# Relative-position attention plus a gated MLP: keys of a head split over the two row halves, scores and transposes in 64-row tiles, double-bank copies, another order

## The chip, the cores and the metric

The kernel runs on one core of a Trainium2 chip. The metric is the device time of one execution in microseconds (us). The profile is one execution of the same program; its time is the span from its first to its last instruction. The engines are named as the profile names them: PE (TensorE matmuls), PEld (TensorE weight loads), DVE (VectorE), ACT (ScalarE), POOL (GpSimd) and SP (the queue that issues most DMAs).

## The reference, cut to what matters

```python
# q, k, v: (8 batches, 8 heads, 576, 64) float32
scores = q @ k^T / 8
x = log1p(|i - j|) / log1p(max(i, 1))              # 576 x 576
scores += (relu(x * w1 + b1) @ w2)[head]           # a bias per head
attn = exp(scores - rowmax); attn /= rowsum + 1e-9
y = attn @ v                                       # -> 4608 tokens x 512
out = ((y @ W1) * (y @ W2)) @ W3 @ W_out           # 512 -> 1024 -> 1024 -> 512
```

All is float32. W3 and W_out are multiplied with each other once (the fold), so that the MLP is an up part (two products) and a down part (one). To get float32 results from one-pass matmuls, an operand is split into a rounded part and a rest (h and l), and a product is the sum of terms such as h*h + h*l + l*h.

## The kernel before, in words

**Stages.** A prologue makes the bias of all heads and stores it in DRAM (nb_d); attention runs over 32 units (4 head pairs times 8 batches, u = 8 * pair + batch); the fold multiplies W3 by W_out; the MLP runs over 9 chunks of 512 tokens. Stages overlap at their ends. While attention runs, W3 and W_out are converted in 24 pieces (steps c0 to c7, units with batch 1 to 6); W1 and W2 are converted in 16 pieces after it.

**One unit** has nine score tiles: 0 to 7 (head h = t mod 2, query rows 128*(t div 2) and on) and M, whose 128 rows are the last 64 query rows of both heads. Its steps, each on one engine:

- ld (SP): raw q, k and v are loaded. g (POOL): q and k are split into h and l parts. gq makes Q, gk makes K and kl.
- S (PE): a tile's 128 x 576 scores, in a PSUM tile `s` of two banks, 288 columns in each; two such tiles exist.
- T (DVE): scores plus bias `nb`, scaled, into `ts`, with the row extreme `mx`. E (ACT): exp into `pp`, with the row sum.
- F (PE): transposes of `pp`, 128 x 128 each, into a PSUM tile `pst`; four one-bank tiles exist. H (DVE or ACT): copies out of `pst` into `pt` and `px`. L and N are the remaining corners.
- r (DVE): reciprocals of the row sums, each unit, transposed in N, stored to DRAM by SP (rd).
- W0, W1 (PE): value products for queries 0 to 255 and 256 to 575, with 64-column tiles: the two heads lie in the two column halves. X: their copies out of PSUM. xd (SP): the unit's result to DRAM.

**Order.** A table (ORDER) gives each step of unit u a time u * PERIOD + t; sorted, this is the order in which PE, DVE, ACT and POOL issue. Each engine runs its list in order and waits at the front. SP's list is sorted by the framework. So a unit's S, the F of the unit before and the W of an earlier one are interleaved. The fold and the MLP are placed the same way after `t_s`, the time of the last S or E.

In `scores` one tile half takes two matmuls: Q holds the h part of q on rows 0 to 63 and the l part on rows 64 to 127, K and kl hold the h and l part of k on both halves, so that all 128 rows add up (h + l) * (h + l).

Of the kernel before, what the change touches and what calls it, by code (L numbers as in the profile page):

```python
# [55 lines left out]
def arrange(NU, pieces):

    at = {n: (t, e) for e, steps in ORDER.items() for n, t in steps.items()}
    at["rd"] = at["HN"][0] + 0.8, "SP"
    at["xd"] = max(at["X0"][0], at["X1"][0]) + 0.8, "SP"  # L60
    at["c0"] = at["c1"][0] - 4.8, "SP"
    at["c7"] = max(at["c2"][0], at["c6"][0]) + 0.6, "POOL"
    return {(n, u): (u * PERIOD + t if u or n not in FIRST else FIRST[n], e) for u in range(NU) for n, (t, e) in at.items() if n[0] != "c" or u in pieces}


@with_exitstack
def relpos_attention_moe(
# [133 lines left out]

    Q2 = []
    for i in range(2):
        qt = qk.tile([P, 2 * (S + P)], F32R, name=f"Q{i}")
        nc.gpsimd.memset(f(qt[:, S:S + P]), 0.0)
        Q2.append(qt)

# [40 lines left out]
    def op_g(u, n):  # L248

        d = st[u]  # L250
        x = d.pop("r" + n)
        if n == "q":
            Q = Q2[u % 2]
            Qd = halves(Q)[:, :, 0:S]
            x = halves(x)
# [1 line left out]
            nc.gpsimd.tensor_tensor(Qd[hi], x[hi], f(Qd[hi]), op=ALU.subtract)
            d["Q"] = Q
        else:
            K = qk.tile([P, 2 * S], F32R, name="K", bufs=2)  # L260
            kl = qk.tile([P, 2 * S], F32R, name="kl", bufs=2)
            nc.gpsimd.tensor_scalar(K, x, 1.0, 1.0, op0=ALU.mult, op1=ALU.mult)
            nc.gpsimd.tensor_tensor(kl, x, f(K), op=ALU.subtract)
            d.update(K=K, kl=kl)

    def op_S(u, t):
# [1 line left out]
        Q, K, kl = d["Q"], d["K"], d["kl"]
        d["s", t] = ps_s.tile([P, 2, 512], F32, name="s")
        for hf in range(2):  # L270
            scores(d["s", t][:, hf, :HS], t, hf, Q, K, kl)

    def scores(s, t, hf, Q, K, kl):
        js = slice(hf * HS, (hf + 1) * HS)
        if t == "M":

            l, m = Q[:, 512:512 + P], Q[:, S + 64:S + 64 + P]
            ops = [(s, l, x[:, js]) for x in (K, kl)]
            if hf == 0:
                ops += [(s, m, x[:, S + 64:S + 64 + HS]) for x in (K, kl)]  # L280
            else:
                ops += [(s[:, 0:512 - HS], m, x[:, S + 64 + HS:2 * S]) for x in (K, kl)]
                ops += [(s[:, 512 - HS:HS], m, x[:, S:S + 64]) for x in (K, kl)]
# [526 lines left out]
```

## Time and profile before

| | |
|---|---|
| time, median of 3 runs | 1242.14 us (1241.1 to 1243.2) |
| span of the profiled execution | 1241.4 us |
| PE busy | 1200.8 us, 97% of the span, 7136 matmuls |
| PEld / DVE / ACT / POOL busy | 956.6 / 656.6 / 603.5 / 390.0 us |
| mean granted TensorE clock | 0.989 |

A row of groups reads: line, engine, operation, output<-inputs, shapes, count | busy time in all, mean ns of one | idle time of the engine ahead of them, and what ended it. A row of the timeline reads: start, length (us), engine, line, operation, count, and in brackets the idle time ahead and what ended it; the length of a matmul or a weight load holds its way through the array, so the distance from one start to the next says how long it holds the engine. A row of stretches reads: from:to, length, then busy time and count of PE, PEld, DVE, ACT and POOL, granted clock, DMA share, GB/s.

### The profile page before, as it was taken

How to read it: one execution, taken by the hardware profiler on the slowest of the kernel's cores; microseconds unless marked ns; L12 is line 12 of the kernel's file. 1: busy time of each engine (PE TensorE's matmuls, PEld its weight loads, DVE VectorE, ACT ScalarE, POOL GpSimd, SP SyncE). 2: the span in 40 equal slices, each digit the busy share in tenths (PEclk: the TensorE clock that was granted, in tenths of full speed). 3: DMA queues.
4: the chain of work that ended last, by engine and by line, in shares of the span. 5: the costliest groups of instructions: out<-in, count | busy, mean ns of one | idle time of the engine just before them, and what ended most of it. 6: DMA issues, size and time to landing. Idle time of an engine off the chain costs nothing. (4 is left out here: it accounts for less than half of the span.)

```text
span 1241.4 us, 19015 instructions
## 1 busy us (share of the span) xinstructions
PE 1200.8 (97%) x7136; PEld 956.6 (77%) x7136; DVE 656.6 (53%) x1380; ACT 603.5 (49%) x1303; POOL 390.0 (31%) x260
## 2 busy tenths in 40 slices
PE   7679999999999999999989999999999999999998
PEld 3168887777778887887768788888888888888887
DVE  8647776777677767776999532222222131313111
ACT  7558887888788877888544321212121212121211
POOL 0436664666456655661654300000000000000000
PEclk9879999999999999999999999999999999999999
DMA  7854446444645463431443220212111110200001
GB/s 215 286 172 143 144 149 204 133 142 145 220 133 152 152 219 120 148 94 54 135 132 117 68 74 29 68 34 65 38 51 51 51 51 35 68 34 1 29 7 34
DMA packets 60795, 130.25 MB, mean 105 GB/s; under 512 B 8992, under 2 KB 18592, under 8 KB 60704
## 3 DMA queue, kind: packets, MB, share of 16 engines
q1 hardware_dynamic: 59408, 127.32, 32.7%
q10 hardware_dynamic: 1296, 1.72, 0.5%
q8 instruction: 56, 0.92, 0.3%
q14 instruction: 35, 0.29, 0.1%
HBM read 99.10 MB, written 29.92 MB: 104 GB/s over the span
## 5 line engine op out<-in xcount | busy, mean ns | idle before, releaser
L298 DVE CUSTOM_DVE_ANT_0 ts<-s,nb 128x576 f32<-128x576 f32 x256 | 184.7, 749 | 148.1 <-ACT pt L363 74.1
L661 PE MATMUL up<-xh,wl 128*128 128x512 f32 x576 | 225.4, 391 | 0.1
L669 DVE TENSOR_TENSOR g<-up,a 128x512 f32<-128x512 f32 x72 | 49.7, 690 | 332.2 <-PE up L661 332.2
L661 PE MATMUL up<-xh,wh 128*128 128x512 f32 x576 | 225.3, 391 | 0.0
L661 PE MATMUL up<-xl,wh 128*128 128x512 f32 x576 | 225.3, 391 | 0.0
L290 PE MATMUL s<-K,Q 128*128 128x288 f32 (+2 forms) x672 | 206.0, 326 | 16.2 <-DVE mx L298 7.6
L321 ACT ACTIVATE pp<-ts,mx 128x576 f32<-128x576 f32 x256 | 196.7, 770 | 39.2 <-DVE mx L298 39.1
L290 PE MATMUL s<-kl,Q 128*128 128x288 f32 (+2 forms) x672 | 182.1, 295 | 0.0
L686 PE MATMUL o<-w3s,gh 128*128 128x512 f32 x576 | 177.8, 390 | 0.0
L666 ACT COPY a<-up 128x512 f32<-128x512 f32 x72 | 42.2, 586 | 247.5 <-PE up L661 247.5
L647 POOL TENSOR_SCALAR xh<-xr 128x512 fp32r<-128x512 f32 x36 | 23.9, 664 | 435.7 <-DVE xr L643 432.5
L290 PEld LDWEIGHTS s<-K,Q 128*128 128x128 f32 x672 | 128.3, 191 | 38.2 <-DVE mx L298 18.0
L355 PE MATMUL pst<-ident,pp 128*128 128x128 f32 x1024 | 152.8, 278 | 0.0
L363 ACT ACTIVATE pt<-pst 128x512 f32<-128x512 f32 x224 | 129.5, 594 | 34.2 <-PE pst L355 29.9
L397 PE MATMUL pst<-pt,rv 128*64 128x320 f32 (+1 forms) x1024 | 138.3, 412 | 0.0
L355 PEld LDWEIGHTS pst<-ident,pp 128*128 128x128 f32 x1024 | 118.8, 141 | 15.2 <-DVE wi L148 11.8
L672 ACT ACTIVATE gh<-g 128x512 fp32r<-128x512 f32 x72 | 45.5, 632 | 172.8 <-DVE g L669 172.8
L290 PEld LDWEIGHTS s<-kl,Q 128*128 128x128 f32 x672 | 129.0, 192 | 0.0
L661 PEld LDWEIGHTS up<-xh,wl 128*128 128x128 f32 x576 | 108.2, 188 | 23.9 <-DVE wl L582 0.5
L661 PEld LDWEIGHTS up<-xl,wh 128*128 128x128 f32 x576 | 108.3, 188 | 23.3
L661 PEld LDWEIGHTS up<-xh,wh 128*128 128x128 f32 x576 | 108.3, 188 | 23.2
L686 PEld LDWEIGHTS o<-w3s,gh 128*128 128x128 f32 x576 | 108.2, 188 | 22.8
(85 smaller groups left out, 1720.3 us busy)
## 6 DMA issues: line engine op xcount, KB each, us to landing
rk<-in_k_dram SPq DMA_DIRECT2D x31, 576.0 KB
rq<-in_q_dram SPq DMA_DIRECT2D x31, 576.0 KB
wi<-in_moe_w_dram SPq DMA_DIRECT2D x32, 512.0 KB
nb_d<-bev SPq DMA_DIRECT2D x36, 295.5 KB
rv<-in_v_dram SPq DMA_DIRECT2D x32, 320.0 KB
x_d<-x SPq DMA_DIRECT2D x32, 288.0 KB
xr<-x_d SPq DMA_DIRECT2D x36, 256.0 KB
rb<-r_d SPq DMA_DIRECT2D x72, 128.0 KB
```

The costliest lines, as they stand in the source:

```text
L290: nc.tensor.matmul(o, l, r, start=(m == 0), stop=(m == len(ops) - 1))
L298: nc.vector.tensor_tensor_reduce(out=halves(ts), in0=d.pop(("s", t))[:, :, :HS], in1=halves(NB[p, t]), op0=ALU.add, op1=ALU.min, scale=-1. ...
L321: nc.scalar.activation(pp, ts, AF.Exp, bias=mx, scale=-1.0, accum_out=d["sum"][:, col:col + 1])
L355: nc.tensor.transpose(ps[:, c * P:(c + 1) * P], x, ident)
L363: nc.scalar.activation(o, x, AF.Copy)
L397: nc.tensor.matmul(acc[rows], x[:, c0:c0 + D], m, start=(c == 0), stop=(c == 4))
L647: nc.gpsimd.tensor_scalar(xh, xr, 1.0, 1.0, op0=ALU.mult, op1=ALU.mult)
L661: nc.tensor.matmul(acc, l[:, cc], r, start=(n == 0), stop=(n == 3 * NC - 1))
L666: nc.scalar.copy(a, ps[0])
L669: nc.vector.tensor_tensor(g, ps[1], a, op=ALU.mult)
L672: nc.scalar.activation(gh, g, AF.Copy)
L686: nc.tensor.matmul(d["o", t], l[:, sl], folded[ft][r], start=(ft == 0 and n == 0), stop=(ft == NF - 1 and n == 2),)
```

## The change

**Operands.** k is no longer doubled: of a head's 576 keys the first 288 lie on rows 0 to 63, the others on rows 64 to 127 (raw k is 128 x 576 in place of 128 x 1152). q lies on both halves, h and l in tiles of their own, with each head padded to 640 columns (128 x 1280). There is one raw buffer of each, where there were two.

**Scores.** A tile is three terms (qh*kh, ql*kh, qh*kl; M six), and each term is two matmuls: rows 0 to 63 write the first bank, rows 64 to 127 the second. The term l*l is left out.

**Transposes.** Each 128 x 128 block is turned by two matmuls of 64 rows, one per bank. `pst` is a two-bank tile; there are two. F0 to F3 turn both heads of a query block (16 matmuls), FL what lies past column 512, FN a corner. H copies 1024 columns at once. W0 and W1 share a `pst` tile from W0's start to X, which is now on DVE.

**Other work.** Row sums of a pair's 8 units are kept in one tile; r, its transpose (R) and its 16 small DMAs come once per pair. In every conversion piece the clamp goes from DVE to POOL and the `rest` step from ACT to POOL. ORDER, PERIOD, the number of buffers and the pace of the fold are others: X and HN follow T7 on DVE, W1 of a unit stands three periods behind its first score tile, the first unit begins with tiles 6 and M.

TensorE at the end of W's neighbourhood, before: a score tile's second half and the next one, transposes, W1 (`s` scores, `pst` transposes or value products).

```order
L290 MATMUL s<-K,Q_121 128x288
L290 MATMUL s<-kl,Q_121 128x288
L290 MATMUL s<-K,Q_121 128x288
L290 MATMUL s<-kl,Q_121 128x288
L355 MATMUL pst<-ident,pp 128x128 x4
L397 MATMUL pst<-pt_857,rv 64x320 x8
L397 MATMUL pst<-px_858,rv 64x320 x2
```

The same place now: F0, S0, W1.

```order
L321 MATMUL pst<-ident,pp 128x64 x16
L266 MATMUL s<-kh,qh 128x288 x2
L266 MATMUL s<-kh,ql 128x288 x2
L266 MATMUL s<-kl,qh 128x288 x2
L386 MATMUL pst<-pt_858,rv 64x320 x8
L386 MATMUL pst<-pt_858,rv 64x256
L386 MATMUL pst<-px_859,rv 64x64
L386 MATMUL pst<-pt_858,rv 64x256
L386 MATMUL pst<-px_859,rv 64x64
```

Four full-row matmuls of a score tile have become three pairs of half-row ones, four transposes sixteen shorter ones, and W1's last part is cut in two.

TensorE further on, now: S4, FN, F3. F3 reuses the `pst` tile that W0 and W1 of another unit filled.

```order
L266 MATMUL s<-kh,qh 128x288 x2
L266 MATMUL s<-kh,ql 128x288 x2
L266 MATMUL s<-kl,qh 128x288 x2
L328 MATMUL pst<-ident,ppM_861 128x64
L329 MATMUL pst<-ident,ppM_861 128x64
L321 MATMUL pst<-ident,pp 128x64 x16
```

F3 thus stands behind the X that empties that tile; ahead of it PE has nothing else in its list.

VectorE around the corner copies (`px`), before (`ts,mx<-s` is a T, its second row reads the row extreme):

```order
L361 COPY pt_859<-pst 128x8x64
L298 ISA ts,mx<-s,nb_4117 128x576
L298 ISA mx 128x1
L298 ISA ts,mx<-s,nb_4167 128x576
L298 ISA mx 128x1
L361 COPY px_860<-pst 64x64 x2
L361 COPY rt<-pst 9x128
L134 TENSOR_SCALAR wmag<-wmag 128x512
```

and now, from T7 to HL:

```order
L277 ISA ts,mx<-s,nb_4623 128x576
L277 ISA mx 128x1
L344 COPY x<-pst 128x256
L344 COPY x<-pst 128x320
L344 COPY px_857<-pst 64x64 x2
L277 ISA ts,mx<-s,nb_4665 128x576
L277 ISA mx 128x1
L277 ISA ts,mx<-s,nb_4763 128x576
L277 ISA mx 128x1
L344 COPY pt_856<-pst 128x2x4x128
```

The two copies of X stand behind T7, HN and T4 behind X; the clamp (L134) has left this list.

```diff
-AT_F, PACE_F = 2.00, 2.80
+AT_F, PACE_F = 2.50, 3.20
-AT_W1, PACE_W, AT_X, PACE_X = 4.00, 5.70, 24.00, 2.10
+AT_W1, PACE_W, AT_X, PACE_X = 4.00, 5.70, 37.00, 2.10
-PERIOD = 15.82
+PERIOD = 13.21
-        "S0": 0.00, "S1": 1.66, "S2": 2.64, "S3": 4.31, "S4": 5.18, "S5": 8.31, "S6": 8.84, "F0": 9.37, "F1": 12.87,
+        "S6": 0.00, "SM": 0.40, "S5": 1.75, "S7": 5.79, "S4": 6.19, "S3": 7.68, "S2": 9.48, "S1": 9.88, "S0": 15.85,
...
+AT_R = 23.41
-NPP, NTS, NPS = 6, 3, 4
+NPP, NTS, NPS = 7, 4, 2
...
         def rest():
-            nc.scalar.activation(x, d["lo"].bitcast(U32), AF.Copy, scale=2.0 ** -52)
+            nc.gpsimd.tensor_scalar(x, d["lo"].bitcast(U32), 2.0 ** -52, 1.0, op0=ALU.mult, op1=ALU.mult)
 
         def clamp():
-            nc.vector.tensor_scalar(d["mag"], d["mag"], LEAST, MOST, op0=ALU.max, op1=ALU.min)
+            nc.gpsimd.tensor_scalar(d["mag"], d["mag"], LEAST, MOST, op0=ALU.max, op1=ALU.min)
...
-    raw = att_r.enter_context(tc.tile_pool(name="raw", bufs=2, side="right"))
+    raw = att_r.enter_context(tc.tile_pool(name="raw", bufs=1, side="right"))
...
+        h = qk.tile([P, x.shape[1]], F32R, name=f"{n}h", bufs=2)
+        l = qk.tile([P, x.shape[1]], F32R, name=f"{n}l", bufs=2)
+        nc.gpsimd.tensor_scalar(h, x, 1.0, 1.0, op0=ALU.mult, op1=ALU.mult)
+        nc.gpsimd.tensor_tensor(l, x, f(h), op=ALU.subtract)
+        d[n] = (h, l)
+
+    TERMS = ((0, 0), (1, 0), (0, 1))
...
-            ops = [(s, l, x[:, h * S + hf * HS:h * S + (hf + 1) * HS]) for x in (K, kl)]
-        for m, (o, l, r) in enumerate(ops):
-            nc.tensor.matmul(o, l, r, start=(m == 0), stop=(m == len(ops) - 1))
+            ops = [(h, h * SQW + i * P, x, y) for x, y in TERMS]
+        for m, (h, q0, x, y) in enumerate(ops):
+            for hf, rows in enumerate((lo, hi)):
+                nc.tensor.matmul(
+                    s[:, hf, :HS], Q[x][rows, q0:q0 + P], K[y][rows, h * HS:(h + 1) * HS],
+                    start=(m == 0), stop=(m == len(ops) - 1),
+                )
...
-            nc.vector.tensor_scalar(r, d["sum"], 1e-9, None, op0=ALU.add)
-            nc.vector.reciprocal(r, r)
+            nc.vector.tensor_scalar(sums[p], sums[p], 1e-9, None, op0=ALU.add)
+            nc.vector.reciprocal(sums[p], sums[p])
...
+    def turn(ps, c0, x):
+        for hf, rows in enumerate((lo, hi)):
+            n = x.shape[1]
+            nc.tensor.transpose(ps[0:n, hf, c0:c0 + 64], x[rows], ident[rows, rows])
 
     def op_F(u, n):
         d = st[u]
-        ps = ps_t.tile([P, 512], F32, name="pst")
+        ps = d["F" + n] = ps_t.tile([P, 2, 512], F32, name="pst")
...
+            for c in range(4):
+                for h in range(2):
+                    c0 = h * (S + 64) + c * P
+                    turn(ps, (2 * c + h) * 64, d["P", int(n)][:, c0:c0 + P])
...
     def op_W(u, n):
...
-        acc = ps_t.tile([P, 512], F32, name="pst")[:, 0:n_q]
+        if "acc" not in d:
+            d["acc"] = ps_t.tile([P, 2, 512], F32, name="pst")
+        acc = d["acc"][:, int(n), 0:qs.stop - qs.start]
```

More of the change, by code (lines that the diff above doesn't have):

```diff
@@ L56, in arrange @@
 def arrange(NU, pieces):
     at = {n: (t, e) for e, steps in ORDER.items() for n, t in steps.items()}
[L59 to L63, printed above, removed]
+    at.update(r=(max(at["E" + t][0] for t in TILES) + 1.0, "DVE"), R=(AT_R, "PE"), HR=(AT_R + 0.85, "DVE"), rd=(AT_R + 1.3, "SP"))
@@ L66, in relpos_attention_moe @@
+    at["xd"] = max(t for n, (t, _) in at.items() if n[0] == "X") + 0.8, "SP"
+    at["c0"] = min(at["c1"][0], at["c2"][0]) - 4.4, "SP"
+    return {(n, u): (u * PERIOD + t if u or n not in FIRST else FIRST[n], e) for u in range(NU) for n, (t, e) in at.items() if (n[0] != "c" or u in pieces) and (n not in ("r", "R", "HR", "rd") or u % 8 == 7)}
 @with_exitstack
@@ L195, in relpos_attention_moe @@
     lo, hi = slice(0, 64), slice(64, 128)
-    NB = {}
+    NB, sums, rts = {}, {}, {}
     st = {u: {"P": [None] * 9} for u in range(NU)}
[L202 to L206, printed above, removed]
     def halves(x):
@@ L238, in load @@
         else:
-            t = raw.tile([P, 2 * S], F32, name=f"r{which}")
+            t = raw.tile([P, src.shape[3]], F32, name=f"r{which}")
         queue = nc.scalar if u == 0 and which != "v" else nc.sync
@@ L266, in op_S @@
+        l = qk.tile([P, x.shape[1]], F32R, name=f"{n}l", bufs=2)
[3 more added lines that the diff above has]
+    TERMS = ((0, 0), (1, 0), (0, 1))
     def op_S(u, t):
         d = st[u]
[L268 to L274, printed above, removed]
-        if t == "M":
[L277 to L283, printed above, removed]
+        Q, K = d["q"], d["k"]
+        s = d["s", t] = ps_s.tile([P, 2, 512], F32, name="s")
+        if t == "M":
+            ops = [(h, h * SQW + 512, x, y) for h in range(2) for x, y in TERMS]
@@ L310, in op_E @@
         ts, mx = d.pop(("t", t))
-        if "sum" not in d:
-            d["sum"] = sm.tile([P, 9], F32, name="sum", bufs=3)
+        p, b = units[u]
+        if p not in sums:
+            sums[p] = sm.tile([P, 9 * B], F32, name="sum")
         if t == "M":
-            pp, col = ppool.tile([P, S], F32, name="ppM", bufs=2), 8
-            d["PM"] = pp
+            pp, col = PM2[u % 2][:, 64:64 + S], 8
         else:
@@ L395, in op_W @@
                 c0 = (4 * h + c if c < 4 else 8 + h) * D
-                m = PT[:, c, h * S + qs.start:h * S + qs.stop] if c < 4 else PX[:, qs]
-                nc.tensor.matmul(acc[rows], x[:, c0:c0 + D], m, start=(c == 0), stop=(c == 4))
+                if c < 4:
+                    ms = [(acc[rows], PT[:, 2 * c + h, qs])]
+                else:
+                    k0, k1 = qs.start // 64, min(qs.stop, 512) // 64
+                    w = (k1 - k0) * 64
+                    ms = [(acc[rows, 0:w].rearrange("p (k j) -> p k j", j=64), PT[:, k0:k1, S:SQW])]
+                    if qs.stop == S:
+                        ms.append((acc[rows, w:], PX))
+                for n_m, (o, m) in enumerate(ms):
+                    nc.tensor.matmul(
+                        o, x[:, c0:c0 + D], m, start=(c == 0), stop=(c == 4 and n_m == len(ms) - 1),
+                    )
         d["acc" + n] = acc
@@ L401, in op_X @@
         d = st[u]
-        if "x" not in d:
-            d["x"] = sm.tile([P, S], F32, name="x")
-        move(on, (d["x"][:, QS[int(n)]], d["acc" + n]))
+        d["x"] = sm.tile([P, S], F32, name="x")
+        move(on, *((d["x"][:, qs], d["acc"][:, m, 0:qs.stop - qs.start]) for m, qs in enumerate(QS)))
     def op_x(u, n):
@@ L549, in relpos_attention_moe @@
     ps_t = att.enter_context(tc.tile_pool(name="ps_t", bufs=NPS, space=PSUM))
-    PTX = [(pt.tile([P, 4, 2 * S], F32, name=f"pt{i}"), pt.tile([P, S], F32, name=f"px{i}")) for i in range(2)]
+    PTX = [(pt.tile([P, 8, SQW], F32, name=f"pt{i}"), pt.tile([P, 64], F32, name=f"px{i}")) for i in range(2)]
+    PM2 = [ppool.tile([P, S + P], F32, name=f"ppM{i}") for i in range(2)]
+    for x in PM2:
+        for c0 in (0, 64 + S):
+            nc.gpsimd.memset(x[:, c0:c0 + 64], 0.0)
     drive([e for e in later if e[0] < t_s])
```

119 lines of the change are left out of this document (54 added, 65 removed), and 5 rows, old and new, of the table ORDER.

## The prediction, made before the changed kernel had run

> **What bounds the kernel now.** I read the stretches first, to see which engine is full in which stage, then the timeline of TensorE in one unit, then the rows of the engines that empty its results.
>
> ```profile
> core 0: 1241.4 us, clock 0.989
> 100.00:200.00 100.00, 99.28 (x784) 80.91 (x783) 74.55 (x184) 79.96 (x185) 61.58 (x37) 1.00 0.55 169
> 580.00:640.00 60.00, 54.40 (x273) 40.83 (x268) 53.49 (x69) 32.74 (x62) 31.38 (x23) 1.00 0.49 142
> 640.00:710.00 70.00, 69.04 (x301) 55.92 (x300) 59.80 (x80) 29.13 (x50) 32.21 (x25) 1.00 0.31 98
> ```
>
> In attention PE is busy for 99.28 of 100 us at full clock, DVE 74.55, ACT 79.96, POOL 61.58: PE alone sets the pace. In the fold (580 to 710) DVE is nearly as full as PE. From 710 on the MLP runs; the change does not touch it.
>
> ```profile
> 300.83 1.95 PE L397 MATMUL pst<-pt,rv 128*64 128x256 f32 x16
> 303.14 0.40 PE L290 MATMUL s<-K,Q 128*128 128x288 f32 x1
> 304.82 2.38 PE L397 MATMUL pst<-pt,rv 128*64 128x320 f32 x16
> 307.67 0.66 PE L355 MATMUL pst<-ident,pp 128*128 128x128 f32 x4
> 309.05 0.38 PE L290 MATMUL s<-K,Q 128*128 128x288 f32 x1
> 309.27 0.30 PE L290 MATMUL s<-kl,Q 128*128 128x288 f32 x1
> 309.40 0.29 PE L290 MATMUL s<-K,Q 128*128 128x288 f32 x1
> 315.92 0.27 PE L342 MATMUL pst<-ident,ppM 128*64 128x128 f32 x1
> 316.03 0.27 PE L343 MATMUL pst<-ident,ppM 128*128 128x128 f32 x1
> 573.65 1.95 PE L397 MATMUL pst<-pt,rv 128*64 128x256 f32 x16
> ```
>
> From start to start: W0 holds PE for 2.31 us, W1 for 2.85, a 288-column score matmul for 0.133 (0.22 as the first after another kind), a transpose for 0.11. From one unit's W0 (300.83) to that of the 17th unit after it (573.65) are 272.82 us: **16.05 us a unit**.
>
> **The change on PE.** A score tile goes from four turns to three pairs. If the two halves of a pair run side by side, it takes 3 x 0.133 = 0.40 us in place of 0.53; all nine (M is double) 4.0. No row of before has 64-row tiles, so this is the first unknown. The nearest rows are those of column halves:
>
> ```profile
> L397 PEld LDWEIGHTS pst<-pt,rv 128*64 128x64 f32 x1024 | 67.8, 136 | 48.8 <-issue 10.5 <-PE wacc L619 0.4
> 57.09 0.23 PE L517 MATMUL bacc<-zact,w2b 128*32 128x16 f32 x1
> 57.10 0.23 PE L517 MATMUL bacc<-zdve,w2b 128*32 128x16 f32 x1
> 309.40 0.19 PEld L290 LDWEIGHTS s<-kl,Q 128*128 128x128 f32 x1
> 310.04 0.19 PEld L290 LDWEIGHTS s<-K,Q 128*128 128x128 f32 x1
> 310.15 0.19 PEld L290 LDWEIGHTS s<-kl,Q 128*128 128x128 f32 x1
> 310.29 0.42 PEld L355 LDWEIGHTS pst<-ident,pp 128*128 128x128 f32 x4
> L355 PEld LDWEIGHTS pst<-ident,pp 128*128 128x128 f32 x1024 | 118.8, 141 | 15.2 <-DVE wi L148 11.8 <-issue 3.4
> L342 PEld LDWEIGHTS pst<-ident,ppM 128*64 128x64 f32 x32 | 3.5, 110 | 0.0
> ```
>
> The value products load 1024 times 136 ns, 139 us, in 67.8 us of busy time: two column halves load at once. Column tiles also start their matmuls 0.01 us apart. The load at 309.40 begins with the matmul of the same rows at 309.40: the next weights come in while the array works. So I take side by side for row halves too. Bounds: one after the other would cost 0.11 to 0.14 per load (310.04, 310.15, 310.29) and no gain at all; below 0.133 a pair cannot go, since its columns are as many as now.
>
> The Trainium skill ("TensorE: Matmul & The Clock Gate", "LDWEIGHTS (loading the stationary operand)") says that a load is paid by its columns, whatever the rows, and its part "Packing small matmuls — row/col tiling" that a load overlaps a running matmul only when the row groups differ. The first speaks against this change: at the page's 128 / 1.2 = 107 ns, the 142 loads of S and F would be 15.2 us a unit if they queue (rival 1). By the second the two halves load side by side, and the sum is mine; but its "only" is contradicted at 309.40, where load and matmul both are of all rows.
>
> A transpose pair streams 64 columns, half of 0.11 us; its 128-column load takes, by the step from 110 ns (64 columns) to 141 (128), 2 x 31 = 62 ns. I take 0.062 per pair: F0 to F3 and FL 0.50 each, 41 pairs 2.5 us, where 39 transposes took 4.3. Bounds 0.055 and 0.11. W0 and W1 stay (5.2), four changes of kind at 0.09 too. PE's work is 4.0 + 2.5 + 5.2 + 0.4 = **12.1 us** a unit.
>
> **What the others need.** PE is then no longer the whole story: the copies are.
>
> ```profile
> 299.77 0.69 DVE L361 COPY pt<-pst 128x512 f32<-128x512 f32 x1
> 300.37 0.75 DVE L298 CUSTOM_DVE_ANT_0 ts<-s,nb 128x576 f32<-128x576 f32 x1
> 305.29 0.75 DVE L298 CUSTOM_DVE_ANT_0 ts<-s,nb 128x576 f32<-128x576 f32 x1
> 305.97 0.69 DVE L143 SCALAR_TENSOR_TENSOR wmag<-wi,wmag 128x512 int32<-128x512 int32 x1
> 312.32 0.42 DVE L361 COPY px<-pst 128x256 f32<-128x256 f32 x1
> 312.65 1.72 DVE L328 TENSOR_SCALAR r<-sum 128x9 f32<-128x9 f32 x1
> L363 ACT ACTIVATE pt<-pst 128x512 f32<-128x512 f32 x224 | 129.5, 594 | 34.2 <-PE pst L355 29.9
> L363 ACT ACTIVATE px<-pst 128x256 f32<-128x256 f32 x32 | 12.2, 380 | 0.0
> L321 ACT ACTIVATE pp<-ts,mx 128x576 f32<-128x576 f32 x256 | 196.7, 770 | 39.2 <-DVE mx L298 39.1
> 310.18 0.28 PE L290 MATMUL s<-kl,Q 128*128 128x64 f32 x1
> 310.60 0.76 DVE L298 CUSTOM_DVE_ANT_0 ts<-s,nbM 128x576 f32<-128x576 f32 x1 [0.23 <-PE s L290]
> ```
>
> A T holds DVE for 0.68 us. A DVE copy is 0.42 at 256 columns, 0.69 at 512, so 0.69 + 2 x 0.27 = 1.23 at 1024; on ACT 0.594 + 2 x 0.214 = 1.02. X is 0.33 and then 0.49. Sums: DVE 9 x 0.68 + 2 x 1.23 + 0.82 + HN under 0.7 + three conversion steps of at most 0.7 = 12.2; ACT 9 x 0.77 + 3 x 1.02 + 0.7 = 10.7. POOL, at 61.58 of 100 us, gains two 512-column steps a piece and loses half of the work on k. None reaches 14. Nothing is charged for the moved clamp and `rest`: POOL has 6 us a unit free; without that cover gq and gk would come late for S6, a microsecond for a microsecond.
>
> **The loop.** Each list is walked in order, as the change part shows it. From a score tile's last matmul to its T 0.3 (310.29 to 310.60), to a copy 0.2 (fewer columns), back to PE 0.05; estimates from those rows. From S6 at 0: SM ends 1.3, T6 frees its tile at 1.5, S5 to 1.9, F0 to 2.4, S0 to 2.8, W1 to 5.8, S7 to 6.3. T7 starts 6.6, **X stands behind it**: 7.3 to 8.1. S4 is done at 6.7 and F3, which needs the tile that X empties, is next: PE stands for 1.4 us. F3 to 8.6, its copy on ACT 8.8 to 9.9 (S3 and F1 lie under it), FL needs that tile: 9.9 to 10.4. HL on DVE 10.6 to 11.85 (S2, S1, F2 under it), W0 needs its tile and its data: 11.9 to 14.2, then S6. **14.2 us a unit**, 2.1 of it PE waiting. Bounds: 13.2 (steps counted start to start, handoffs halved), 15.4 (transposes at 0.11 a pair, which adds 0.4 at F0, F3 and FL).
>
> **Ends of the stage.**
>
> ```profile
> 47.20 4.51 POOL L262 TENSOR_SCALAR K<-rk 128x1152 fp32r<-128x1152 f32 x1 [45.65 <-DMA rk<-in_k_dram]
> 63.21 0.61 PE L290 MATMUL s<-K,Q 128*128 128x288 f32 x1 [5.82 <-POOL Q L257]
> 72.44 0.54 SPq L226 DMA_DIRECT2D nb<-nb_d  x1
> 78.10 0.76 DVE L298 CUSTOM_DVE_ANT_0 ts<-s,nb 128x576 f32<-128x576 f32 x1 [4.61 <-DMA nb<-nb_d]
> 582.99 0.28 PE L290 MATMUL s<-kl,Q 128*128 128x64 f32 x1
> 586.73 0.49 PE L619 MATMUL wacc<-woh,w3h 128*128 128x512 f32 x1 [0.87 <-ACT w3h L610]
> ```
>
> Start: PE's list holds bias products behind the first scores, and those waited for POOL until 63.21. POOL now makes k and q of the first unit ahead of the second's, and k is half as wide; by the same rates its first k and q take 8 us of the 16 that ran from 47.20. The first T now needs the bias of the last rows, which landed at 78.10: 70 now, tile M's 2 later. The first three periods lack W and other F (8, 9.5 and 10.5 us by the same walk, from 69), so the fourth starts near 97 (92 to 101).
>
> Pair ends, three times: the bias for tiles 4 and 6 is issued behind the q load, which waits for POOL until 10.7 of the period, and took 5.66 us from issue to T (72.44 to 78.10). It lands at 18.2, where T6 is due at 15.0: 3.2 us. The reciprocals of a pair, 1.72 us on DVE ahead of T4 and HL, cost about 1.2 four times, R and its copy 0.3. Together 16 us.
>
> The last S then ends at 97 + 29 x 14.2 + 16 + 3 = 528, where it ends at 583 now. More is left by then: five W's and all F of the last unit, 15.7 us of PE work in place of 8.6 (W0, W1 and 31 transposes), so 7 go back; two more for the wider gap ahead of the first fold matmul (583 to 586.73 now). The fold is else the same work on PE, with DVE relieved. 583 - 528 - 7 - 2 = 46 us. 1241.4 - 46 = 1195.4 for a profiled execution; the median of the runs shown is 0.7 above its span: **1196 us**.
>
> **Rivals.**
>
> 1. Row halves load and run one after the other. For: no row shows them side by side, and loads of 128 columns are seen no closer than 0.11. Against: the column halves. Scores 60 loads x 0.107 = 6.4, transposes 82 x 0.062 = 5.1, W 5.2, changes 0.4: 17.1 a unit on PE. 97 + 496 + 10 + 3 = 606, so 23 + 7 + 2 later: 1274 us, slower. It decides once a score pair takes over 0.19 us: 30 pairs x 0.06 bring the loop to 16.
> 2. Scores pair up, transposes stay at 0.11 or two-bank copies take longer than the slope says: 15.4 a unit, 35 us more: 1231.
> 3. Handoffs are shorter than read, so that the loop is near 13.2: 29 us less, 1167. For: the 0.2 and 0.05 are estimates. Against: X, H3 and HL stay in a row.
> 4. What attention gains is lost in the fold, where DVE is busy for 53.49 of 60 and 59.80 of 70 us. Against: the fold only starts earlier, and the clamps leave DVE. It would need an idle stretch of 46 us; 1242.
>
> **How the numbers follow.** The loop as walked 0.62 (own range 1175 to 1216, from the ends of the start, the pair ends and half a microsecond a unit), rival 2 0.14, rival 3 0.13, rival 1 0.09, rival 4 0.02. The range takes in 2 and 3: 1165 to 1231. Faster by over 0.2% (2.5 us, about what this kernel's timing tells): 0.89; same 0.02; slower 0.09.
>
> **What would show it.** Half-row score matmuls that start 0.01 apart with 0.133 to the next pair, and PE idle ahead of F3 with X as its releaser, 1 to 2 us a unit; waits on ACT ahead of FL and on DVE ahead of W0; W0 to W0 14.2 us; DVE waiting 3 us for `nb` three times; the last score near 528. Wrong would be a full PE (rival 1), a loop that closes elsewhere (POOL late with k, ACT late with H3), or an MLP that starts with a gap.

## The result: slower by 1.2%

The changed kernel takes 1257.5 us (median of 4 runs, 1256.9 to 1257.8) where the kernel before takes 1242.7 (4 runs, 1241.1 to 1243.5): a ratio of 1.0121, with a 95% interval of 1.0107 to 1.0136. Forecast were 1196 us, with a range of 1165 to 1231.

The profiled execution has a span of 1255.9 us. The first lines of its page:

```profile
span 1255.9 us, 22540 instructions
PE 1132.2 (90%) x9092; PEld 881.3 (70%) x9092; DVE 638.9 (51%) x1288; ACT 521.4 (42%) x1039; POOL 452.1 (36%) x342
```

PE is busy for 68.6 us less than before (1200.8), and yet the kernel is longer. So PE does less and waits more. The stretches say where (busy time and count of PE, PEld, DVE, ACT, POOL, then the granted clock, the DMA share and GB/s):

```profile
100.00:200.00 100.00, 84.03 (x1181) 64.86 (x1179) 71.40 (x170) 66.98 (x138) 69.09 (x48) 0.97 0.49 162
...
600.00:640.00 40.00, 25.30 (x100) 18.07 (x97) 29.80 (x38) 10.97 (x19) 27.67 (x22) 0.89 0.50 152
640.00:710.00 70.00, 62.67 (x245) 48.38 (x245) 52.66 (x61) 20.15 (x34) 48.69 (x39) 0.92 0.30 95
```

In attention PE has 16 us of 100 free, about as forecast. In the fold and the start of the MLP, where it was nearly full before (54.40 of 60, 69.04 of 70), it now stands for 15 us of 40 and 7 of 70, at a granted clock of 0.89 to 0.92.

**The loop of attention is the one that was forecast, 0.5 us longer.** TensorE in one unit, from W0 to W0 (start, length, count, and what ended the idle time ahead):

```profile
289.54 2.38 PE L386 MATMUL pst<-pt,rv 128*64 128x256 f32 x20
291.85 0.40 PE L266 MATMUL s<-kh,qh 64*128 64x288 f32 x2
292.09 0.30 PE L266 MATMUL s<-kh,ql 64*128 64x288 f32 x2
292.22 0.29 PE L266 MATMUL s<-kl,qh 64*128 64x288 f32 x2
292.36 0.29 PE L266 MATMUL s<-kh,qh 64*128 64x288 f32 x2
...
300.40 0.68 PE L321 MATMUL pst<-ident,pp 64*128 64x64 f32 x15 [1.34 <-DVE x L344]
...
304.26 2.38 PE L386 MATMUL pst<-pt,rv 128*64 128x256 f32 x20
```

Two halves come as one row "x2", and from 292.09 to 292.22 to 292.36 a pair holds PE for 0.13 us: the row halves do run side by side. F3 waits 1.34 us for X (1.4 was forecast). From 289.54 to 304.26 are 14.72 us, where 14.2 stood in the forecast and 16.05 before.

**The pair ends cost more.** From W0 to W0 across a pair end pass 22.7, 22.3 and 22.1 us. SP's issues and DVE at the second one, and then PE:

```profile
302.82 0.33 SPq L237 DMA_DIRECT2D rq<-in_q_dram  x1
303.24 0.39 SPq L223 DMA_DIRECT2D nb<-nb_d  x1
...
304.23 0.86 SPq L398 DMA_DIRECT2D x_d<-x  x1
305.19 0.38 SPq L221 DMA_DIRECT2D nb<-nb_d  x1
```

```profile
312.37 0.76 DVE L277 CUSTOM_DVE_ANT_0 ts<-s,nb 128x576 f32<-128x576 f32 x1 [5.67 <-DMA nb<-nb_d]
```

```profile
307.74 0.29 PE L266 MATMUL s<-kl,qh 64*128 64x288 f32 x2
313.19 0.61 PE L266 MATMUL s<-kh,qh 64*128 64x288 f32 x2 [5.15 <-DVE mx L277]
313.59 0.45 PE L266 MATMUL s<-kh,ql 64*128 64x288 f32 x2
313.83 0.45 PE L266 MATMUL s<-kl,qh 64*128 64x288 f32 x2
```

The bias of tiles 4 and 6 (the issue at 305.19) stands behind q, the bias of tiles 5 and 7 and the unit's result; it lands at 312.3. PE stands for 5.15 us. After that a pair takes 0.24 us (313.59 to 313.83) in place of 0.13, and the granted clock is 0.50 from 313 to 317, 0.92 in the next microsecond and 1.00 from 318 on: some 4 us of work at half rate, about 2 us lost (an estimate), so an idle stretch is paid for twice. The Trainium skill ("TensorE: Matmul & The Clock Gate", "Part 1: The HAM clock gate") has this as a clock at half rate, 1.2 GHz, after an idle window of some 3.4 us. By that rate 288 columns take 0.24 us, an estimate, and the trace agrees here.

**The stage after attention.** POOL while the weights of the MLP are converted, one piece and the start of the next (L131 is `rest`, L134 the clamp):

```profile
643.09 0.78 POOL L131 TENSOR_SCALAR w<-wi 128x512 f32<-128x512 uint32 x1 [2.10 <-DMA wi<-in_moe_w_dram]
643.95 1.97 POOL L134 TENSOR_SCALAR wmag<-wmag 128x512 f32<-128x512 f32 x1
645.89 1.29 POOL L151 TENSOR_TENSOR w<-w,wi 128x512 f32<-128x512 f32 x1
647.27 1.36 POOL L152 TENSOR_TENSOR w<-wmag,w 128x512 f32<-128x512 f32 x1
650.90 0.67 POOL L131 TENSOR_SCALAR w<-wi 128x512 f32<-128x512 uint32 x1 [2.28 <-DMA wi<-in_moe_w_dram]
```

From the start of one piece to the next are 7.81 us: L151 is the last to read `wi` and ends at 647.18, the next transfer is issued at 647.22, lands 3.7 us later, and POOL needs 4.1 us before L151 has ended again. From the first to the last L152 the 16 pieces take 8.5 us each (582.09 to 709.89), where they took 6.8 before (598.80 to 700.88). In the chain of work that ended last between 500 and 712, the transfers of `wi` have the largest share (15.0%) and POOL's clamp the next (11.4%).

A table of all kernels serves for the comparisons below. The columns come from PE's timeline: W0 to W0 of an ordinary unit (median), the three distances across a pair end, the start of the last score matmul, and the rest of the span after it, all of one profiled execution per kernel.

| kernel | unit | pair ends | last score | rest of span |
|---|---|---|---|---|
| before | 16.05 | 16.0, 16.0, 16.0 | 583.0 | 658.4 |
| the change | 14.72 | 22.7, 22.3, 22.1 | 558.2 | 697.7 |
| e1: 16 pieces back | 14.72 | 21.8, 22.7, 21.7 | 559.0 | 677.0 |
| e2: SP in list order | 14.72 | 15.6, 15.6, 16.7 | 536.6 | 697.2 |
| e3: X ahead of T7 | 13.34 | 17.7, 16.5, 18.5 | 507.5 | 697.5 |
| e4: all on one row half | 23.96 | 24.6, 24.5, 24.5 | 830.3 | 698.0 |
| e5: e1, e2 and e3 | 13.79 | 19.6, 15.9, 17.8 | 517.5 | 678.2 |
| e6: before, steps to POOL | 16.04 | 16.0, 16.0, 16.1 | 582.7 | 681.6 |
| e7: clamp alone back | 14.72 | 22.1, 22.8, 20.8 | 553.2 | 682.6 |
| e8: 24 pieces back | 14.61 | 22.8, 21.9, 22.4 | 557.7 | 696.5 |
| e9: e1 and e3 | 13.34 | 17.4, 16.5, 17.1 | 505.7 | 678.6 |
| e10: e9, bias by ACT | 13.33 | 16.8, 15.5, 15.7 | 509.8 | 676.8 |
| e11: e9, chunk loads later | 13.33 | 15.6, 17.8, 17.2 | 505.1 | 670.0 |
| e12: scores on one half | 17.39 | 23.5, 23.8, 20.8 | 669.5 | 696.7 |

The last column is the main thing to see: whatever attention takes, the rest of the span is 696.5 to 698.0 us in each of the six kernels (the change itself, e2, e3, e4, e8 and e12) that leave both steps of the 16 pieces on POOL, 677 to 679 in the four that only put them back (e1, e5, e9, e10), and 658 before. What attention gains is carried to the end in full; the loss is made afterwards, anew. The column of the last score is less steady: e7, whose edit lies behind attention, has it 5 us earlier than the change, 3.6 of them at the first W0.

### The profile page after: what moved, and what is told of

It is laid out like the page before. It is cut to its first block, busy times and chain, and to the rows that moved or that the text cites. A ratio compares the mean times of both kernels' runs of the same rounds, so it can differ in the third digit from the quotient of the medians.

```text
span 1255.9 us, 22540 instructions
## 1 busy us (share of the span) xinstructions
PE 1132.2 (90%) x9092; PEld 881.3 (70%) x9092; DVE 638.9 (51%) x1288; ACT 521.4 (42%) x1039; POOL 452.1 (36%) x342
## 4 chain that ended last, share of the span: by engine, by line
PE 72%; DVE 7%; POOL 6%; DMA 6%; ACT 4%; issue 3%; SPq 1%; ACTq 0%; DVEq 0%; POOLq 0%
PE up L652 29%; PE o L677 15%; PE pst L386 12%; PE s L266 8%; PE pst L321 5%; DVE ts L277 4%; ACT pt L346 3%; DMA wi<-in_moe_w_dram 3%; PE bacc L504 2%; POOL wmag L134 2%; DVE x L344 2%; DMA nb_d<-bev 1%; DMA nb<-nb_d 1%; PE pst L332 1%; POOL w L151 1%
## 5 line engine op out<-in xcount | busy, mean ns | idle before, releaser
L277 DVE CUSTOM_DVE_ANT_0 ts<-s,nb 128x576 f32<-128x576 f32 x256 | 188.4, 753 | 131.5 <-PE s L266 95.9
L677 PE MATMUL o<-w3s,gh 128*128 128x512 f32 x576 | 180.6, 395 | 3.7 <-ACT gh L663 3.7
L638 POOL TENSOR_SCALAR xh<-xr 128x512 fp32r<-128x512 f32 x36 | 23.8, 662 | 437.8 <-DVE xr L634 436.3
L386 PE MATMUL pst<-pt,rv 128*64 128x256 f32 (+1 forms) x1280 | 171.0, 413 | 0.5 <-DVE rt L344 0.5
L266 PE MATMUL s<-kh,qh 64*128 64x288 f32 x640 | 118.7, 363 | 34.5 <-DVE mx L277 31.9
L321 PE MATMUL pst<-ident,pp 64*128 64x64 f32 x2304 | 108.3, 226 | 40.7 <-DVE x L344 39.8
L346 ACT ACTIVATE pt<-pst 128x1024 f32<-128x1024 f32 x96 | 96.2, 1025 | 95.1 <-PE pst L321 95.1
L321 PEld LDWEIGHTS pst<-ident,pp 64*128 64x128 f32 x2304 | 100.2, 141 | 47.9 <-issue 44.9
L386 PEld LDWEIGHTS pst<-pt,rv 128*64 128x64 f32 x1280 | 89.1, 139 | 63.3 <-issue 9.7
L677 PE MATMUL o<-w3s,gl 128*128 128x512 f32 x288 | 114.5, 398 | 3.6 <-DVE gl L666 3.6
L266 PEld LDWEIGHTS s<-kh,qh 64*128 64x128 f32 x640 | 64.6, 194 | 58.9 <-DVE mx L277 41.6
```

The lines of the kernel that those rows point to most:

```text
L266: nc.tensor.matmul(s[:, hf, :HS], Q[x][rows, q0:q0 + P], K[y][rows, h * HS:(h + 1) * HS], start=(m == 0), stop=(m == len(ops) - 1),)
L277: nc.vector.tensor_tensor_reduce(out=halves(ts), in0=d.pop(("s", t))[:, :, :HS], in1=halves(NB[p, t]), op0=ALU.add, op1=ALU.min, scale=-1. ...
L321: nc.tensor.transpose(ps[0:n, hf, c0:c0 + 64], x[rows], ident[rows, rows])
L346: nc.scalar.activation(o, x, AF.Copy)
L386: nc.tensor.matmul(o, x[:, c0:c0 + D], m, start=(c == 0), stop=(c == 4 and n_m == len(ms) - 1),)
L677: nc.tensor.matmul(d["o", t], l[:, sl], folded[ft][r], start=(ft == 0 and n == 0), stop=(ft == NF - 1 and n == 2),)
```

## The experiments

### e1: the 16 MLP pieces as before

```
+            if pieces > 1:
+                nc.scalar.activation(x, d["lo"].bitcast(U32), AF.Copy, scale=2.0 ** -52)
+            else:
                 nc.gpsimd.tensor_scalar(x, d["lo"].bitcast(U32), 2.0 ** -52, 1.0, op0=ALU.mult, op1=ALU.mult)
...
+            if pieces > 1:
+                nc.vector.tensor_scalar(d["mag"], d["mag"], LEAST, MOST, op0=ALU.max, op1=ALU.min)
+            else:
                 nc.gpsimd.tensor_scalar(d["mag"], d["mag"], LEAST, MOST, op0=ALU.max, op1=ALU.min)
```

> The changed kernel, but in the 16 pieces of the MLP weights (those that are converted after attention) the clamp is back on DVE and the multiply `rest` back on ACT; the 24 pieces inside attention stay as in the change. Theory A: the stage after the last score tile is set by the loop transfer of wi, rest (0.75) and clamp (1.97) on POOL, wi free, next transfer, 7.8 us a piece where before it was 6.2; with it undone the stage from the last score (554) to the end falls from 702 us towards the 658 of before: span 1215 to 1232. Theory B: the stage is longer because more attention work (W and F) is left over, or because of the transfers of wi themselves (3.6 us each): the span stays above 1250. The period of attention, 14.7 us, is the same by both.

1234.9 us, ratio to before 0.9949 (0.9929 to 0.9969); span of the profiled execution 1236.0. The rest of the span falls by 20.7 us, attention stays. (The last score matmul of the change starts at 558.2; the 554 of the expectation was a few tiles early.) It goes part of the way that theory A gave it: 677.0 is not 658, and 1236 is above A's range. A stretch of e1:

```profile
640.00:710.00 70.00, 69.19 (x302) 56.24 (x301) 52.12 (x68) 25.51 (x44) 26.87 (x21) 1.00 0.27 83
```

From 640 on PE is full again. Between 600 and 640 it still stands, in one piece; PE and ACT of e1:

```profile
616.65 0.79 PE L616 MATMUL wacc<-woh,w3h 128*128 128x512 f32 x1 [8.05 <-ACT w3h L607]
```

```profile
614.87 0.66 ACT L128 ACTIVATE wmag<-wi 128x512 f32<-128x512 f32 x1 [9.48 <-DMA wi<-in_moe_w_dram]
```

The fold waits for w3h, w3h stands in ACT's list behind the first step of a piece, and that waits for its `wi`. e11 takes this up.

### e6: the two steps moved, in the kernel before

```
-            nc.scalar.activation(x, d["lo"].bitcast(U32), AF.Copy, scale=2.0 ** -52)
+            nc.gpsimd.tensor_scalar(x, d["lo"].bitcast(U32), 2.0 ** -52, 1.0, op0=ALU.mult, op1=ALU.mult)
...
-            nc.vector.tensor_scalar(d["mag"], d["mag"], LEAST, MOST, op0=ALU.max, op1=ALU.min)
+            nc.gpsimd.tensor_scalar(d["mag"], d["mag"], LEAST, MOST, op0=ALU.max, op1=ALU.min)
```

> The kernel before with one part of the change alone: clamp and `rest` of all 40 pieces on POOL. Theory A: the part costs what undoing it for the 16 MLP pieces gave back, 20 us, and nothing in attention, where PE stays full: span 1256 to 1266 against 1241. Theory B: the 20 us came only from the meeting of the part with the larger rest of attention; here it costs under 5 us.

1264.7 us, ratio 1.0183 (1.0167 to 1.0198). Attention is not touched (16.04 us a unit, last score at 582.7), and the rest of the span grows by 23.2 us. So this one part of the change costs 21 to 23 us by itself, with or without the other parts. Theory A.

Why it costs so much, the groups show. First the kernel before, from 583 to 720:

```profile
L137 DVE TENSOR_SCALAR wmag<-wmag 128x512 int32<-128x512 int32 x16 | 17.0, 1063 | 0.3
L134 DVE TENSOR_SCALAR wmag<-wmag 128x512 f32<-128x512 f32 x16 | 17.0, 1060 | 0.5 <-ACT wmag L128 0.5
L143 DVE SCALAR_TENSOR_TENSOR wmag<-wi,wmag 128x512 int32<-128x512 int32 x16 | 15.7, 980 | 0.3
L148 DVE TENSOR_SCALAR wi<-wmag 128x512 int32<-128x512 int32 x16 | 7.1, 444 | 0.0
```

Then the change, in the same stretch:

```profile
L134 POOL TENSOR_SCALAR wmag<-wmag 128x512 f32<-128x512 f32 x14 | 27.8, 1986 | 1.5 <-ACT wmag L128 0.7
L137 DVE TENSOR_SCALAR wmag<-wmag 128x512 int32<-128x512 int32 x14 | 19.7, 1409 | 15.2 <-POOL wmag L134 15.2
L143 DVE SCALAR_TENSOR_TENSOR wmag<-wi,wmag 128x512 int32<-128x512 int32 x15 | 18.5, 1233 | 0.2
L148 DVE TENSOR_SCALAR wi<-wmag 128x512 int32<-128x512 int32 x15 | 10.3, 689 | 0.0
```

DVE is rid of a clamp of 1.06 us a piece, but its three other steps take 3.33 us together (1.409, 1.233 and 0.689) in place of 2.49: of the 1.06 only 0.22 is left. And the clamp takes 1.99 us on POOL.

### e7: only the clamp back

```
+            if pieces > 1:
+                nc.vector.tensor_scalar(d["mag"], d["mag"], LEAST, MOST, op0=ALU.max, op1=ALU.min)
+            else:
                 nc.gpsimd.tensor_scalar(d["mag"], d["mag"], LEAST, MOST, op0=ALU.max, op1=ALU.min)
```

> The changed kernel with the clamp alone back on DVE in the 16 MLP pieces; `rest` stays on POOL there. Theory A: what counts is the clamp, 1.97 us on POOL against 0.67 to 1.06 on DVE, and the slower DVE steps beside it (1.41, 1.23 and 0.69 where they took 1.06, 0.98 and 0.44): most of the 21 us comes back, span 1236 to 1243. Theory B: `rest` on POOL counts as much, since it stands first behind the transfer of wi: span 1244 to 1252.

1241.6 us, ratio 0.9998 (0.9984 to 1.0011). The rest of the span is 682.6: the clamp accounts for 15.1 of the 20.7 us, `rest` for the other 5.6. Both count, the clamp more, as theory A had it.

### e8: the 24 pieces inside attention as before

```
-            if pieces > 1:
+            if pieces == 1:
```

(against e1, at both places)

> The changed kernel with clamp and `rest` back on DVE and ACT in the 24 pieces inside attention, and left on POOL in the 16 MLP pieces. Theory A: in attention POOL has 5 us a unit free and no step of the loop waits for it: 14.7 us a unit as now, span 1252 to 1259. Theory B: POOL's clamp delays gq and gk or slows DVE's T beside it: 14.4 us a unit or less, span 1247 or less.

1255.7 us, ratio 1.0119 (1.0097 to 1.0141), which is the change's own. A unit takes 14.61 us, 0.11 less, and the rest 696.5. Theory A: inside attention the same two steps cost at most 0.11 us a unit, and the time does not show it.

### e2: SP's transfers in the order of the list

```
-    drive([e for e in later if e[0] < t_s])
+    drive([e for e in later if e[0] < t_s], mybir.EngineType.SP)
```

SP joins the engines whose order is kept as written (`drive` hands the second argument on; that part is left out here).

> The changed kernel, but SP's transfers of the attention stage are kept in the order in which the program's list emits them, so that at a pair's end the bias of tiles 4 and 6 is issued ahead of the next q, not behind it. Theory A: the 22.4 us between the W0 of two units at the three pair ends are the 14.7 of a unit and the late landing of that bias (issued 305.19, landed 312.3, T6 wanted it at 306.7); issued at 302.5 it lands near 307 and the three come to 17 to 18 us, 14 us less in all; attention's end moves by as much and the span goes to 1239 to 1246. Theory B: the transfers are limited by the bytes in flight (2 MB at 400 GB/s), so the order only decides which of them is late: three pair ends still over 21 us and the span within 3 us of 1256.

1236.8 us, ratio 0.9958 (0.9944 to 0.9971). At the second pair end SP now issues:

```profile
289.62 0.38 SPq L221 DMA_DIRECT2D nb<-nb_d  x1
290.88 0.33 SPq L237 DMA_DIRECT2D rq<-in_q_dram  x1
```

and DVE no longer waits for a transfer:

```profile
295.47 0.76 DVE L277 CUSTOM_DVE_ANT_0 ts<-s,nb 128x576 f32<-128x576 f32 x1 [0.68 <-ACT pp L300]
```

The three pair ends fall from 7.4 to 7.9 us over a unit to 0.9, 0.9 and 1.9, 19.3 us in all, and the start (first W0 at 99.5 in place of 103.0) gives 3.5 more; a few of the units between became longer, and the last score comes 21.6 earlier. Theory A was right on the cause, and its 14 us were too few: it left 17 to 18 us at a pair end, where 15.6 to 16.7 remain, and had no term for the slower clock behind the idle stretch. The run is also a bound for what the once-a-pair reciprocals and R cost: at most 0.9 us at a pair end.

### e3: X ahead of T7

```
-        "c5": 16.70, "c6": 17.40, "T0": 17.48, "HN": 21.15, "HL": 23.20, "H2": 26.18, "X": 46.49,
+        "c5": 16.70, "c6": 17.40, "T0": 17.48, "HN": 21.15, "HL": 23.20, "H2": 26.18, "X": 46.40,
```

> The changed kernel with one number changed: DVE's copy X of the value products stands ahead of T7 in DVE's list, not behind it. Theory A (the loop as predicted): F3 waits 1.3 us for X because X stands behind T7; X then ends 0.7 us earlier, F3, H3, FL, HL and W0 follow, T7 comes 0.8 us later and with it S4's tile, which lies beside H3. A unit falls from 14.7 to 13.7 to 14.1 us and the span by 18 to 29 us: 1227 to 1238. Theory B: T7 and T4 become late instead, since S4, S3 and S2 wait for the tiles that T7 and T4 free: 14.6 us or more a unit, span 1254 or more.

1207.9 us, ratio 0.9732 (0.9716 to 0.9748). One number in a table makes the slower kernel a faster one. DVE, and TensorE beside it:

```profile
347.47 0.82 DVE L344 COPY x<-pst 128x256 f32<-128x256 f32 x2 [0.72 <-PE pst L386]
348.21 0.75 DVE L277 CUSTOM_DVE_ANT_0 ts<-s,nb 128x576 f32<-128x576 f32 x1
```

```profile
344.46 2.86 PE L386 MATMUL pst<-pt,rv 128*64 128x320 f32 x20
...
348.44 0.71 PE L321 MATMUL pst<-ident,pp 64*128 64x64 f32 x16
```

X starts as soon as W1 is done, F3 follows S7, S4 and FN with no wait, and T7, now second, holds nothing up. A unit takes 13.34 us. 29 units at 1.38 us make 40 us, the pair ends give 10.3, and the last score comes 50.6 us earlier. This is theory A's mechanism, at nearly its full 1.4 us; I had set 0.6 to 1.0 for fear of what T7 would delay. Why the pair ends shrink as well was not looked into.

### e4 and e12: both halves on the same rows

```
-                    s[:, hf, :HS], Q[x][rows, q0:q0 + P], K[y][rows, h * HS:(h + 1) * HS],
+                    s[:, hf, :HS], Q[x][lo, q0:q0 + P], K[y][lo, h * HS:(h + 1) * HS],
...
-                    turn(ps, (2 * c + h) * 64, d["P", int(n)][:, c0:c0 + P])
+                    turn(ps, (2 * c + h) * 64, d["P", int(n)][:, c0:c0 + P], (lo, lo))
```

e4 has both edits, e12 the first alone (`turn` takes the rows as a further argument; that part is left out here). Both kernels leave half of the keys out of the result.

> The changed kernel, but both matmuls of every score pair, and both transposes of every pair of F0 to F3, take rows 0 to 63 (the other half of the keys and of the scores is left out of the result; the number and the shapes of the instructions are the same). Theory A: halves run side by side only because they lie on different rows; on the same rows a score pair takes two turns, 0.24 to 0.27 us in place of 0.133, and a transpose pair 0.11 to 0.14 in place of 0.03 to 0.06: 3.6 + 2 to 4 us more PE work a unit, PE becomes full and a unit takes 17 to 20 us: span 1330 to 1420. Theory B: the pairs overlap by the pipeline alone, whatever their rows: 0.133 a pair as now and the span within 5 us of 1256.

1532.3 us, ratio 1.2343 (1.2318 to 1.2367). Score pairs of e4, in two places of one unit, and two stretches:

```profile
350.89 0.42 PE L266 MATMUL s<-kh,ql 64*128 64x288 f32 x2
351.15 0.42 PE L266 MATMUL s<-kl,qh 64*128 64x288 f32 x2
...
367.15 0.68 PE L266 MATMUL s<-kl,qh 64*128 64x288 f32 x2
367.63 0.68 PE L266 MATMUL s<-kh,qh 64*128 64x288 f32 x2
```

```profile
100.00:200.00 100.00, 96.19 (x730) 84.21 (x729) 48.51 (x109) 46.26 (x94) 45.35 (x33) 0.70 0.25 79
300.00:400.00 100.00, 96.21 (x774) 81.85 (x771) 47.89 (x110) 43.15 (x88) 45.32 (x32) 0.79 0.27 85
```

On the same rows a pair takes 0.26 us, two turns: theory A, so it is the different rows that let the halves run together, not the pipeline. The part "Packing small matmuls — row/col tiling" of the Trainium skill's page "TensorE: Matmul & The Clock Gate" says the same, and here the trace bears it out. But the unit came to 24.0 us, beyond A's 17 to 20: at times a pair takes 0.48 us, and the granted clock is 0.70 to 0.79, though PE is busy for 96 of 100 us. PE's work at full clock is 12.1 us, 4.0 more for the scores and 2.5 more for the transposes, 18.6 (an estimate), and 18.6 over 0.77 are 24. The 0.79 is a mean of two values: in the unit shown the clock is 1.00 from 351 to 363, among scores and transposes on one half, then 0.50 until W0, whose matmuls use all rows, has run for some 2.5 us. e12 asked which of the two edits brings the low clock:

> The changed kernel with both matmuls of every score pair on rows 0 to 63 (the other half of the keys is left out of the result), the transposes as in the change. With scores and transposes on the same rows a unit took 24.0 us where 18.6 us of PE work at full clock were expected; the granted clock was 0.70 to 0.81 there. Theory A: the low clock comes with the score pairs on the same rows; with them alone PE has 12.1 + 4.0 = 16.1 us a unit at full clock, and again a clock under 0.85 makes 19 to 21 us of it: span 1390 to 1450. Theory B: it came with the transposes, so here the clock stays over 0.95 and a unit takes 16.5 to 17.8 us: span 1310 to 1350.

1368.6 us, ratio 1.1010 (1.0978 to 1.1042).

```profile
100.00:200.00 100.00, 95.23 (x926) 83.25 (x924) 58.83 (x136) 55.02 (x112) 56.24 (x41) 0.81 0.30 95
300.00:400.00 100.00, 92.69 (x958) 76.64 (x957) 57.33 (x138) 53.87 (x110) 49.40 (x35) 0.91 0.40 128
```

It falls between the two theories: a clock of 0.81 to 0.91 and 17.4 us in an ordinary unit (some take 19 to 20). With fewer pairs on one half the clock is less low. What sets it stays open.

### e5, e9, e10, e11: what the parts give together

e5 is e1, e2 and e3 at once; e9 is e1 and e3; e10 and e11 are e9 with one edit more each.

> The three edits at once: clamp and `rest` of the 16 MLP pieces back on DVE and ACT, SP's transfers of attention in the order of the list, X ahead of T7. One by one they gave 21, 20 and 48 us of a span of 1256. Theory A: they lie in stages that follow each other (the unit, the pair ends, the stage after the last score), so they add, less the part of the pair ends that X had already taken (with X ahead three ends cost 4.4, 3.1 and 5.2 us over a unit, not 7.7): 21 + 48 + 10 = 79, span 1172 to 1182. Theory B: with attention 60 us earlier the stage after it meets a bound of its own (its transfers of wi, or the fold on PE), and the sum is lost there: span 1190 or more.

1196.6 us, ratio 0.9639 (0.9611 to 0.9668); span 1195.7. It misses theory A's 1172 to 1182, and not for B's reason either: the rest of the span gave its 20 us (678.2). Attention is what became longer, with the last score at 517.5 where X alone had 507.5. e9 leaves SP's order out:

> Two of the three edits: X ahead of T7, and clamp and `rest` of the 16 MLP pieces back on DVE and ACT; SP as in the change. Theory A: in the sum of three, 10 us were lost because SP's list order made the units longer (last score 517.5, where X alone had 507.5) while the stage after it gave its whole 20 us (1195.7 - 517.5 = 678 against 697); without that order the last score is back at 507 to 508 and the span 1184 to 1188. Theory B: the loss comes from the stage after attention, which cannot start earlier than its transfers: span 1193 or more.

1183.5 us, ratio 0.9527 (0.9510 to 0.9543), last score 505.7, span 1184.3. Theory A. With X ahead of T7, SP's list order costs some 12 us (517.5 against 505.7 at the last score); in the change itself it gave 21. Why it turns is not shown.

e10 sends the next pair's bias from ACT's queue (each transfer of `load_bias` then goes through `queue`):

```
     def load_bias(p, ts):
+        queue = nc.sync if p == 0 else nc.scalar
...
```

> As the run with X ahead of T7 and the 16 pieces back, and the bias of the second to fourth pair is issued from ACT's queue, not from SP's behind the next q. Theory A: the three pair ends come from 17.7, 16.4 and 18.5 us down to 14 to 15 and the span falls by 6 to 10 us more: 1176 to 1181. Theory B: ACT pays 0.4 to 0.6 us for each of seven issues, 3 to 4 us at each pair end while ACT is 75% busy, so nothing is left of it: within 3 us of the run without it.

1188.7 us, ratio 0.9573 (0.9557 to 0.9589): 5 us worse than e9. The pair ends fall by 3.0 us in all, but the first W0 comes 1.9 us later and the units between grow from 13.45 to 13.65 in the mean. Theory B's "nothing is left of it" is nearest, but neither theory gave a loss, and where it comes from is not shown.

e11 takes up the idle stretch of e1:

```
-    put(later, load_x(0), end + 0.5)
+    put(later, load_x(0), end + 6.0)
```

> As the run with X ahead of T7 and the 16 pieces back, and the loads of the first MLP chunk stand 5.5 us later in the list, so that the transfer of the next wi goes ahead of them on SP. Theory A: the idle stretch of 8 us in the middle of the fold (PE waits for w3h, ACT for the wi that SP holds back behind 12 loads) shrinks below 3 us and the span by 5 to 8 us. Theory B: the chunk's own loads then come late for the first up products: no gain, within 3 us of the run without it.

1177.5 us, ratio 0.9483 (0.9463 to 0.9503), the fastest of the kernels here. In e9 the idle stretch is still there; in e11 ACT's wait for `wi` at this place and the fold behind it are short. First PE of e9, then ACT and PE of e11:

```profile
565.03 0.80 PE L616 MATMUL wacc<-woh,w3h 128*128 128x512 f32 x1 [8.19 <-ACT w3h L607]
```

```profile
553.64 0.67 ACT L128 ACTIVATE wmag<-wi 128x512 f32<-128x512 f32 x1 [2.15 <-DMA wi<-in_moe_w_dram]
```

```profile
555.46 0.50 PE L616 MATMUL wacc<-woh,w3h 128*128 128x512 f32 x1 [0.72 <-ACT w3h L607]
```

8 us of idle PE have become 0.72, and the rest of the span is 670.0, 8.6 less than in e9. The medians of four runs lie 6.1 us apart (1183.5 and 1177.5), so 6 is the safer figure. Theory A.

## Why the prediction was wrong, step by step

The forecast span was 1195.4, the measured one 1255.9: 60.5 us too few. By the forecast's own split, 30.2 of them lie before the last score (528 forecast, 558.2 measured) and 30.3 after it (667.4 forecast, 697.7 measured). Either half alone would have left the span near 1226, still shorter than before; it took both.

- **"So I take side by side for row halves too": right.** 0.13 us a pair, 0.5 to 0.6 for 16 transposes; e4 shows that rival 1's premise, one after the other, does hold as soon as the rows are the same.
- **"The loop": right in its steps, 0.5 us short.** Each link stands where the walk had it: X behind T7, F3 waiting for X (1.34 us), H3, FL, HL, W0. Counted from S6, S7 comes at 6.1 (forecast 5.8), X at 7.6 (7.3), F3 at 8.6 (8.1), HL at 11.1 (10.6), W0 at 12.4 (11.9): the difference is there by F3, and 0.4 of it already at W1's start (3.2, forecast 2.8), so it lies in the scores, F0 and the waits ahead of W1. 29 units make 15 us of it. e3 confirms the loop from the other side: without the one wait the unit is 1.38 us shorter.
- **"Start ... near 97": 8 us short.** The fourth period starts at 105.3. The first T was right, but tile M's came at 74.7, not 72 (rows behind this list), and the first three periods (from one T of tile M to the next) took 8.9, 11.1 and 12.9 us in place of 8, 9.5 and 10.5. PE also stood for 5.15 and 4.21 us there, and its pairs take 0.24 us from 70.6 to 84.8. SP's order is 3.5 of the 8 (e2); for the others no run was made.
- **"Pair ends": right in mechanism, too small.** The bias did come late behind q, but by 5.67 us on DVE and not 3.2, and the clock fell behind the idle stretch. The forecast had it land at 18.2 of the period, though its own terms, 10.7 and 5.66, make 16.4. Measured from S6 (291.85), q was issued at 11.0 (forecast 10.7), the bias at 13.3, and it took 7.1 us to land, with 2.1 MB issued on SP between 302.82 and 305.19. Measured 23.0 us over the three, forecast 16. The share that I gave to the reciprocals was too large. The 1.72 us of the row at 312.65 are mostly a wait: that instruction ends with POOL's of 2.67 us, which runs from 311.68 to 314.35 in the kernel before, and the shortest of its 32 takes 0.17 us. Here the one for a whole pair (L305) takes 0.19.
- **"Nothing is charged for the moved clamp and `rest`": the step that failed.** For the 24 pieces inside attention next to nothing was indeed due (e8). The row of 1.72 us could have warned: DVE waits there beside a long POOL instruction. But the same function converts 16 pieces after attention, where POOL, DVE and the transfers of `wi` run in a chain per piece, and I did not look for the cover there. That is 20.7 us (e1), 23.2 in the kernel before (e6).
- **"The fold is else the same work on PE, with DVE relieved": failed with it.** DVE's relief was 0.22 us a piece, since its other steps slowed beside POOL. And PE's own work being the same was no argument in a stage where it waits for others. The 9 us for the work left over fit: with e1's steps back and e11's order the rest of the span is 670.0, against 667.4. No run shows them alone.
- **Of what remains after attention, 6 to 8.6 us** are SP's order again (e11 against e9, by medians and by profiles): `wi` behind twelve loads of the first MLP chunk, ACT behind `wi`, the fold behind ACT. The forecast had no term for it.
- **Rival 4, "what attention gains is lost in the fold", came nearest, and had 0.02.** The last score is 24.8 us earlier than before, and the span behind it 39.3 longer. It was put away with "needs an idle stretch of 46 us" and "the clamps leave DVE". The first was the wrong test: it needs no single stretch, 1.3 to 1.7 us on each of 16 pieces and a slower clock did it, together with the late start and the pair ends. Rivals 2 and 3 did not occur; 13.3 us a unit, near rival 3's number, was reached only with X ahead of T7 (e3, e9 to e11), and not by shorter handoffs.

The two T's of the start, on DVE of the change:

```profile
69.37 0.76 DVE L277 CUSTOM_DVE_ANT_0 ts<-s,nb 128x576 f32<-128x576 f32 x1 [18.88 <-DMA nb<-nb_d]
74.67 0.76 DVE L277 CUSTOM_DVE_ANT_0 ts<-s,nbM 128x576 f32<-128x576 f32 x1 [4.53 <-DMA nbM<-nb_d]
```

What had been named as the sign of a wrong forecast was partly there: the loop closed where it should and PE was not full, while the fold had gaps. Three quarters of the missing 60 us came from terms outside the loop: I had walked the order row by row only for one unit in the middle.

## What to carry to other kernels

When a change moves a step to another engine inside a shared helper, price it at every place that calls the helper, and above all where an engine runs a chain with single transfers; an engine that is free on average gives no cover there. One position in a list can be worth more than the whole rearrangement of the work: X and T7 gave 50 us here, the bias and q 21, `wi` and the chunk's loads 6. Such gains need not add: with X first, the order of SP that gave 21 us in the change cost 12. A gain early in a program is kept to the end only if the later stage does not change with it: read the time from the last instruction of one stage to the end as a number of its own.
